# Retention and mixture of experts on one core: y turned in 64x64 quarters of the array, with the order of the loop's VectorE work changed

## The chip, the core and the metric

The kernel runs on one core of a Trainium2 chip. A core has five engines that run side by side, each with its own in-order queue: TensorE (PE, matmuls, with weight loads shown as PEld), VectorE (DVE), ScalarE (ACT), GpSimd (POOL) and SyncE (SP, which here issues most DMAs). Matmuls write to PSUM, everything else lives in SBUF, and 16 DMA engines move data from and to HBM. The metric is the device time of one execution in microseconds.

## The reference, cut to what matters

Inputs: q, k, v of shape (4 batches, 8 heads, 768 steps, 64), a gate of 512 x 8, a noise gate of the same shape, noise, and for 8 experts w1 (512 x 1024) and w2 (1024 x 512), all float32.

```python
# retention with decay: per head h, gamma = 1 - 2 ** (-5 - h)
for t in range(S):
    state = gamma * state + k[t] (x) v[t]            # 64 x 64 per batch and head
    y[t] = (1 / sqrt(64)) * q[t] @ state
x = y.transpose(0, 2, 1, 3).reshape(3072, 512)       # one row per token
# noisy top-2 gating
noisy = x @ w_gate + log1p(exp(x @ w_noise)) * noise
top2 = argpartition(-noisy, 2)[:, :2]; weights = softmax of the two
# experts
for e in range(8):
    out[mask] += weight * (relu(x[mask] @ w1[e]) @ w2[e])
```

## The kernel before

The retention is cut into 24 chunks of 128 steps (`NCH`; 6 chunks per batch, `NC`), and a loop over chunks j does for all 8 heads:

- `qk(j + 1)`: the scores k^T q of the next chunk, 8 float32 matmuls in 64-row tiles, into two PSUM tiles `pA`; VectorE multiplies them with the causal mask into `am`, at the end of `qk` (line 356).
- `x_turn(j - 1)`: the y of the chunk before stands in SBUF as `yt`, with features on partitions and steps along the free dimension. Four matmuls with y as the weights (128x128) and a constant `turn` as the moving operand (144 columns: an identity of 128 and 16 gate columns) put tokens on partitions and give the parts of the logits as well. Behind them four matmuls of one column with bf16 squares `sq` give each token's sum of squares.
- `y_state(j)`: the part of y that comes from the state, 8 matmuls in 64x64 quarters of the array, absent in the first chunk of a batch.
- `x_scale(j - 1)`: two short VectorE operations that make a power of two from the sum of squares (`p2m`, `xsa`).
- `mid[j]`: routing work put in by hand for this chunk (lists filled with `P(j, ...)`), mainly VectorE: top-2 search, one-hot tables, the low halves of w1 (`w_lo_half`), and the DMA transposes `x_t` on SP.
- `load(j + 4)`: q, k, v and kt of chunk j + 4, four DMAs of 256 KB on SP. q is scaled by GpSimd (`q_scale`, two chunks ahead), v as well (`v_scale`, one chunk ahead).
- `x_split(j - 1)`: ScalarE writes the scaled x in f16 and copies the logits' parts, VectorE writes the low half, SP stores both to `xbuf`.
- `todo[j]`: more work put in by hand (loads of weights, gathers of x rows on GpSimd).
- `y_mm(j)`: masked scores times v, 8 matmuls of 128x64; ScalarE copies y to `yt`; 8 matmuls `pU` for the state's update (absent in the last chunk of a batch); ScalarE copies the state to U and squares yt into `sq`.

All engines keep the order of the program text (`tc.manual_schedule()`); semaphores only hold an instruction back. PSUM tiles of the loop (`pY`, `pT`) have one buffer each, `pA` two. The gather of the first expert's rows needs an index that VectorE writes in chunk 18 (`slots`), gathers stand in the `todo` of 18 to 20, and the transposes `x_t` of the gathered rows in 20 and 21. Behind the loop the last turn stands among the first expert's matmuls, and the experts follow, with float16 high and low parts (three matmuls for one product).

## Time and profile before

| | |
|---|---|
| median of 3 runs | 645.42 us (645.26 to 645.45) |
| profiled execution | 645.07 us, its span 643.1 us |
| PE | busy 634.6 us (99%), 4919 matmul records |
| PEld, DVE, ACT, POOL | 390.2, 287.1, 299.8, 202.8 us |
| granted clock of PE | 0.998 of full speed |
| DMA | 113.02 MB, mean 176 GB/s |

The span goes from the first to the last instruction of one profiled execution. A matmul on float32 leaves two records. Busy times of records that overlap are counted once; times on PE are ends that are modelled, starts are read. An idle time on an engine other than PE matters only if PE ends up waiting for it.

### The profile page before, as it was taken

The page shows a single profiled execution, that of the slowest core. Times are in us where ns is not written, and L with a number is a line of the kernel's source. Part 1 is how long each engine was busy: PE and PEld are TensorE (multiplying, and loading weights), DVE is VectorE, ACT ScalarE, POOL GpSimd, SP SyncE. Part 2 cuts the span into 40 slices and gives each one's busy share as a digit, 9 for nine tenths or more (in the row PEclk, how much of TensorE's full clock was granted, in tenths as well). Part 3 has the DMA queues.
Part 4 walks back from the last instruction along what each step waited for, and adds up shares of the span by engine and source line. Part 5 has one row for each costly group of instructions (what it writes and reads, how often), then busy time and mean ns, then how long its engine had stood idle before and what let it go on. Part 6 is the DMA issues. An engine that isn't in the chain of part 4 may idle for free.

```text
span 643.1 us, 12254 instructions
## 1 busy us (share of the span) xinstructions
PE 634.6 (99%) x4919; PEld 390.2 (61%) x4919; DVE 287.1 (45%) x740; ACT 299.8 (47%) x559; POOL 202.8 (32%) x166
## 2 busy tenths in 40 slices
PE   9999999999999999999999999999999999999995
PEld 6999998559578544554455445544554465455574
DVE  4678785897454221654162226222622262215020
ACT  6577457615552443554354344434543454344121
POOL 4555472041540134104410433043304320430214
PEclk9999999999999999999999999999999999999999
DMA  8999999988768067736774577447654794572303
GB/s 301 391 391 375 321 314 277 368 194 296 167 127 276 10 124 131 238 79 97 143 205 131 100 129 203 142 87 130 190 162 83 126 209 144 95 126 45 50 10 43
DMA packets 94423, 113.02 MB, mean 176 GB/s; under 512 B 60662, under 2 KB 61820, under 8 KB 90780
## 3 DMA queue, kind: packets, MB, share of 16 engines
q1 hardware_dynamic: 82576, 85.57, 43.6%
q0 software_dynamic: 11776, 26.63, 22.9%
q8 instruction: 40, 0.66, 0.4%
q14 instruction: 19, 0.16, 0.1%
q10 hardware_dynamic: 12, 0.01, 0.0%
HBM read 72.66 MB, written 26.42 MB: 154 GB/s over the span
## 4 chain that ended last, share of the span: by engine, by line
PE 97%; ACT 1%; DVE 1%; issue 0%; POOL 0%; POOLq 0%; ACTq 0%
PE pH L873 13%; PE pH L874 13%; PE pH L875 13%; PE pO L919 12%; PE pO L921 12%; PE pO L920 12%; PE pA L353 4%; PE pT L401 4%; PE pY L375 4%; PE pT L975 2%; PE pY L368 2%; PE pO L963 2%; PE pU L384 1%; PE pO L951 1%; PE pO L950 1%; PE pO L949 1%
## 5 line engine op out<-in xcount | busy, mean ns | idle before, releaser
L910 POOL DMA_INDIRECT out<-ot,idx x51 | 83.6, 1639 | 321.6 <-ACT ot L905 190.2
L873 PE MATMUL pH<-xe,w1h 128*128 128x384 f16 (+5 forms) x576 | 180.9, 314 | 0.0
L875 PE MATMUL pH<-xe,w1l 128*128 128x384 f16 (+5 forms) x576 | 180.9, 314 | 0.0
L874 PE MATMUL pH<-xe,w1h 128*128 128x384 f16 (+5 forms) x576 | 180.8, 314 | 0.0
L882 DVE SCALAR_TENSOR_TENSOR hl<-pH,hh 128x384 f16<-128x384 f32 (+5 forms) x144 | 75.6, 527 | 139.7 <-ACT hh L879 139.0
L921 PE MATMUL pO<-w2h,hl 128*128 128x512 f16 x344 | 130.4, 379 | 0.0
L920 PE MATMUL pO<-w2l,hh 128*128 128x512 f16 x344 | 130.4, 379 | 0.0
L919 PE MATMUL pO<-w2h,hh 128*128 128x512 f16 x344 | 130.4, 379 | 0.0
L879 ACT ACTIVATE hh<-pH 128x384 f16<-128x384 f32 (+5 forms) x144 | 67.1, 467 | 122.7 <-PE pH L875 111.4
L905 ACT ACTIVATE ot<-pO,gse 128x512 f32<-128x512 f32 x45 | 30.9, 687 | 155.2 <-PE pO L921 140.5
L235 DVE SCALAR_TENSOR_TENSOR w1l<-wst,wsc,w1h 128x1024 f16<-128x1024 f32 x28 | 35.9, 1284 | 95.6 <-ACT w1h L230 95.6
L873 PEld LDWEIGHTS <-w1h 128*128 128x128 f16 x576 | 56.3, 98 | 33.0 <-issue 2.7
L875 PEld LDWEIGHTS <-w1l 128*128 128x128 f16 x576 | 56.3, 98 | 30.9
L874 PEld LDWEIGHTS <-w1h 128*128 128x128 f16 x576 | 56.3, 98 | 29.8
L207 ACT ACTIVATE junk<-wst 128x1024 bf16<-128x1024 f32 x64 | 67.2, 1050 | 0.0
L723 POOL DMA_INDIRECT xg<-xbuf,idx x54 | 55.2, 1022 | 30.8 <-issue 12.7
L921 PEld LDWEIGHTS <-hl 128*128 128x128 f16 x344 | 33.7, 98 | 40.6
L919 PEld LDWEIGHTS <-hh 128*128 128x128 f16 x344 | 33.7, 98 | 40.5 <-issue 0.4
L920 PEld LDWEIGHTS <-hh 128*128 128x128 f16 x344 | 33.7, 98 | 39.6
L356 DVE TENSOR_TENSOR am<-pA,mask 128x512 f32<-128x512 f32 x48 | 30.8, 683 | 17.9 <-PE pA L353 17.9
L326 POOL TENSOR_TENSOR vp<-in_v,cs 128x512 f32<-128x512 f32 x24 | 25.1, 1046 | 36.4 <-issue 22.9
L230 ACT ACTIVATE w2h<-wst,wsc 128x1024 f16<-128x1024 f32 x32 | 36.5, 1140 | 0.0
(181 smaller groups left out, 680.5 us busy)
## 6 DMA issues: line engine op xcount, KB each, us to landing
wst<-w SPq DMA_DIRECT2D x28, 1024.0 KB
in_q<-qT SPq DMA_DIRECT2D x24, 256.0 KB
in_k<-kT SPq DMA_DIRECT2D x24, 256.0 KB
in_v<-vt SPq DMA_DIRECT2D x24, 256.0 KB
in_kt<-kt SPq DMA_DIRECT2D x24, 256.0 KB
xbuf<-x SPq DMA_DIRECT2D x24, 256.0 KB
out<-zero SPq DMA_DIRECT2D x6, 1024.0 KB
wst<-w SPq DMA_DIRECT2D x8, 512.0 KB
```

What stands on the lines that cost most here:

```text
L207: nc.scalar.activation(junk, st[:, i * 1024:(i + 1) * 1024], AF.Square, accum_out=ss[:, i:i + 1])
L230: nc.scalar.activation(hi, st[:, i * 1024:(i + 1) * 1024], AF.Copy, scale=sc[:, 0:1])
L723: nc.gpsimd.indirect_dma_start(out=x[:n], out_offset=None, in_=xbuf[:128 + B0 * S] if e == 0 and t < 3 else xbuf, in_offset=bass.IndirectO ...
L873: nc.tensor.matmul(p[:, :n], whi, xh, start=(k == 0), stop=False)
L874: nc.tensor.matmul(p[:, :n], whi, xl, start=False, stop=False)
L875: nc.tensor.matmul(p[:, :n], wlo, xh, start=False, stop=(k == KT - 1))
L879: nc.scalar.activation(hh[:, f, n0:n1], p, AF.Relu)
L882: nc.vector.scalar_tensor_tensor(hl[:, f, n0:n1], p, 0.0, hh[:, f, n0:n1], op0=OP.max, op1=OP.subtract)
L910: nc.gpsimd.indirect_dma_start(out=out, out_offset=bass.IndirectOffsetOnAxis(ap=idx[:n, i:i + 1], axis=0), in_=ot[:n], in_offset=None, com ...
L919: nc.tensor.matmul(p, a, WT["2h"][:, f, :], start=(f == 0), stop=False)
L920: nc.tensor.matmul(p, a, WT["2l"][:, f, :], start=False, stop=False)
L921: nc.tensor.matmul(p, c, WT["2h"][:, f, :], start=False, stop=(f == FT - 1))
```

## The change

The turn of y is done in 64x64 quarters: 16 matmuls, each with a 64x64 piece of y as weights and 80 columns of `turn` (64 of an identity, 16 of the gate); for each of four pieces the two row halves and two column halves of the array. The sums of squares are issued ahead of them, and the squares are made right behind `yt`, before the state's copy. The columns of x come in another order, which w1's rows follow (`PERMX`), and the logits come in four parts instead of two. The masks leave `qk` and stand behind `x_scale`; `mid` stands behind `x_split`. Five low halves of w1 move to other chunks.

```diff
-XW = 128 + 2 * E
+XW = 64 + 2 * E
+PERMX = PERM.reshape(KT, 2, 64).transpose(1, 0, 2).reshape(-1)
 def turn_ident(v):
-            nc.vector.tensor_copy(t[:, :, k, k * 2 * E:k * 2 * E + 128], ident[:, None, :].to_broadcast([128, 2, 128]))
+            nc.vector.tensor_tensor(t[:, :, k, k * 2 * E:k * 2 * E + 64], ident[:, None, :64].to_broadcast([128, 2, 64]),
+                                    ident[:, None, 64:].to_broadcast([128, 2, 64]), op=OP.add)
 def turn_gate(v):
-            nc.vector.tensor_copy(t[:, :, k, 128 - k * 128:XW - k * 128], w[:, :, k])
+            nc.vector.tensor_copy(t[:, :, k, 64 - k * 64:XW - k * 64], w[:, :, k])
 def qk(j):
-        for s in range(2):
-            nc.vector.tensor_tensor(AM[j][:, s], pA[s], mask[:, None, :].to_broadcast([128, HP, C]), op=OP.mult)
+        return pA
+
+    def masked(j, pA, s):
+        nc.vector.tensor_tensor(AM[j][:, s], pA[s], mask[:, None, :].to_broadcast([128, HP, C]), op=OP.mult)
 def y_mm(j):
         nc.scalar.activation(y.rearrange("p (s x) -> p s x", s=2), PY.pop(j)[:, :, :2 * C], AF.Copy)
+        SQ[j] = loads.tile([128, KT, C], BF, name="sq", bufs=1)
+        nc.scalar.activation(SQ[j].rearrange("p n c -> p (n c)"), y, AF.Square)
         if c < NC - 1:
...
             nc.scalar.activation(U[(c + 1) % 2], pU, AF.Copy)
-        SQ[j] = loads.tile([128, KT, C], BF, name="sq", bufs=1)
-        nc.scalar.activation(SQ[j].rearrange("p n c -> p (n c)"), y, AF.Square)
 def x_turn(j):
-        PT[j] = p = t[:, 512 - 2 * XW:512 + 2 * XW]
-        p = p.rearrange("p (s x) -> p s x", s=2)
-        PT[j, "s"] = t[:, 512 + 2 * XW:513 + 2 * XW]
-        y = YT.pop(j)
-        for s in range(2):
-            for g in range(2):
-                nc.tensor.matmul(p[:, s, g * 128:g * 128 + XW], y[:, s, g, :], turn[:, v, 2 * s + g],
-                                 start=(g == 0), stop=True, skip_group_check=True)
+        PT[j] = p = t[:, 512 - 4 * XW:512 + 4 * XW]
+        PT[j, "s"] = t[:, 512 + 4 * XW:513 + 4 * XW]
         q = SQ.pop(j)
         for n in range(KT):
             nc.tensor.matmul(PT[j, "s"], q[:, n], oneb[:, 0:1], start=(n == 0), stop=(n == KT - 1), skip_group_check=True)
-        PT[j, "y"] = PT[j].rearrange("p (n x) -> p n x", x=XW)[:, :, :128]
+        y = YT.pop(j)
+        for n in range(KT):
+            for h in range(2):
+                o = (4 * h + n // 2 * 2) * XW + n % 2 * 64
+                r = slice(h * 64, h * 64 + 64)
+                for m in range(2):
+                    i = slice(m * 64, m * 64 + 64)
+                    nc.tensor.matmul(p[i, o:o + XW], y[r, n // 2, n % 2, i], turn[r, v, n],
+                                     start=(n == 0), stop=True, skip_group_check=True)
+        PT[j, "y"] = PT[j].rearrange("p (n x) -> p n x", x=XW)[:, :, :64]
 def logits(j):
-        nc.scalar.activation(LG[g, "s"][:, j - c0], p.rearrange("p (s x) -> p s x", s=2)[:, :, 128:XW], AF.Copy)
+        nc.scalar.activation(LG[g, "s"][:, j - c0], p.rearrange("p (s x) -> p s x", s=4)[:, :, 64:XW], AF.Copy)
 def route_x(g, c0, c1):
-        ls = LG[g, "s"][:, c0:c1]
-        nc.vector.tensor_tensor(LG[g][:, c0:c1], ls[:, :, 0], ls[:, :, 1], op=OP.add)
+        nc.vector.tensor_reduce(LG[g][:, c0:c1], LG[g, "s"][:, c0:c1].rearrange("p n s e -> p n e s"),
+                                axis=AX.X, op=OP.add)
-    for i, j in ((0, 10), (2, 10), (1, 11), (4, 11), (3, 12), (6, 12), (5, 19), (7, 19)):
+    for i, j in ((0, 10), (2, 10), (4, 11), (6, 12), (1, 18), (3, 19), (5, 19), (7, 21)):
         P(j, w_lo_half, 0, "1", i)
 the loop over j:
+        more = j + 1 < NCH
+        pA = qk(j + 1) if more else None
         if j:
             x_turn(j - 1)
         y_state(j)
...
         if j:
             x_scale(j - 1)
-        for f, a in mid.get(j, []):
-            f(*a)
+        if more:
+            masked(j + 1, pA, 0)
+            masked(j + 1, pA, 1)
         if j < NC - 3:
             q_table(j + 3)
         if j + AHEAD < NCH:
             load(j + AHEAD)
         if j:
             x_split(j - 1)
+        for f, a in mid.get(j, []):
+            f(*a)
         for f, a in todo.get(j, []):
             f(*a)
         y_mm(j)
```

## Rows read from the trace of the kernel before

**Rows 1.** The page's chain that ended last, its shares of the span by engine:
```profile
PE 97%; ACT 1%; DVE 1%; issue 0%; POOL 0%; POOLq 0%; ACTq 0%
```

**Rows 2.** PE's timeline, iteration 13: start us, length us, engine, line, operation:
```profile
62.07 1.16 PE L353 MATMUL pA<-qs,in_k 64*128 64x128 f32 x16
63.17 1.24 PE L401 MATMUL pT<-turn,yt 128*128 128x144 f32 x8
64.25 0.24 PE L405 MATMUL pT<-oneb,sq 128*128 128x1 bf16 x4
64.42 0.67 PE L368 MATMUL pY<-qs,U 64*64 64x128 f32 x16
65.02 1.09 PE L375 MATMUL pY<-am,vp 128*64 128x128 f32 x16
65.94 0.64 PE L384 MATMUL pU<-vp,in_kt 128*64 128x64 f32 x16
66.51 0.72 PE L353 MATMUL pA<-qs,in_k 64*128 64x128 f32 x8
```

**Rows 3.** Table by stage: stretch, its length, busy us (records), clock, DMA share, GB/s:
```profile
30.00:50.00 20.00, 20.00 (x335) 18.15 (x336) 14.23 (x52) 14.56 (x34) 10.33 (x10) 1.00 1.05 390
...
103.00:108.00 5.00, 4.76 (x78) 4.36 (x80) 2.86 (x9) 3.77 (x9) 0.10 (x1) 1.00 1.24 216
108.00:110.00 2.00, 2.00 (x41) 1.57 (x38) 1.79 (x12) 1.29 (x5) 0.11 (x1) 1.00 1.02 389
```

**Rows 4.** PE's timeline, the state part's first three and first four records:
```profile
64.42 0.33 PE L368 MATMUL pY<-qs,U 64*64 64x128 f32 x3
...
64.42 0.34 PE L368 MATMUL pY<-qs,U 64*64 64x128 f32 x4
```

**Rows 5.** PE's timeline: scores of chunks 11 and 21, iteration 12, the expert's first matmul:
```profile
49.83 1.16 PE L353 MATMUL pA<-qs,in_k 64*128 64x128 f32 x16
...
59.33 1.25 PE L401 MATMUL pT<-turn,yt 128*128 128x144 f32 x8
...
60.59 0.98 PE L375 MATMUL pY<-am,vp 128*64 128x128 f32 x14
...
92.97 1.16 PE L353 MATMUL pA<-qs,in_k 64*128 64x128 f32 x16
...
109.73 0.34 PE L873 MATMUL pH<-xe,w1h 128*128 128x384 f16 x1
```

**Rows 6.** ScalarE's timeline where a batch ends (chunk 11): y's copy and its squares:
```profile
58.36 0.60 ACT L379 ACTIVATE yt<-pY 128x512 f32<-128x512 f32 x1 [0.43 <-PE pY L375]
58.99 0.63 ACT L388 ACTIVATE sq<-yt 128x512 bf16<-128x512 f32 x1
```

**Rows 7.** SP's timeline: the issue of chunk 11's q and the eighth issue behind it:
```profile
39.88 0.40 SPq L266 DMA_DIRECT2D in_q<-qT  x1
...
46.47 0.33 SPq L266 DMA_DIRECT2D in_kt<-kt  x1
```

**Rows 8.** GpSimd's timeline: the scaling of q of chunks 11 and 21:
```profile
46.53 1.28 POOL L334 TENSOR_TENSOR qs<-in_q,gq 128x512 f32<-128x512 f32 x1
...
90.60 1.27 POOL L334 TENSOR_TENSOR qs<-in_q,gq 128x512 f32<-128x512 f32 x1
```

**Rows 9.** VectorE's timeline, iteration 16, and the gather's index in iteration 18:
```profile
77.12 1.29 DVE L356 TENSOR_TENSOR am<-pA,mask 128x512 f32<-128x512 f32 x2 [1.15 <-PE pA L353]
...
78.65 0.26 DVE L535 TENSOR_TENSOR posb<-pR,t 128x108 f32<-128x108 f32 x1
...
80.66 0.74 DVE L431 SCALAR_TENSOR_TENSOR x<-pT,xsa,x 128x512 f16<-128x512 f32 x1
...
87.69 0.16 DVE L636 SCALAR_TENSOR_TENSOR idx<-roww 128x3 int32<-128x3 f32 x1
```

**Rows 10.** SP's timeline: the first and the last transpose of the first gathered rows:
```profile
94.87 1.35 SPq L741 DMA_TRANSPOSE xe<-xg  x1
...
102.31 2.22 SPq L741 DMA_TRANSPOSE xe<-xg  x1
```

## The prediction, written before the changed kernel ran

> **What bounds the kernel now.** I read the chain of waits first: 97% of the profiled execution hangs on TensorE (PE) [rows 1]. So a change pays only by what it takes off PE's queue, and only as long as nothing else becomes late there. Then I followed one iteration of the attention loop on PE's timeline [rows 2]: scores `qk`, turn of y (8 records in 1.24 us, since a float32 matmul leaves two), the squares' sums, state part, mask part, state update, next `qk`. Each block begins where the one before ends; the iteration is 66.51 - 62.07 = 4.44 us. [...] Last, the table by stage: from 30 to 50 us PE is busy all of 20 us, but the DMA engines are full as well (share 1.05, 390 GB/s) [rows 3]. That is the second bound, hidden just behind the first.

> **The turn itself.** Before, the stretch from the start of the turn to the state part is 64.42 - 63.17 = 1.25 us [rows 2]. What would 16 quarter matmuls, that is 32 records, take? The trace has quarters already: the state part is 64x64 with 128 columns. Four of its records are over after 0.34 us [rows 4] and all sixteen after 0.67 [rows 2], so a round of four costs 0.33/3 = 0.11. The state update has 64 columns, two tiles side by side, eight rounds within 0.64 [rows 2]; less the last round's tail (0.34 - 0.11 = 0.23 in the state part) that is 0.41/7 = 0.06 a round. Between 64 and 128 columns, 80 come to 0.06 + 0.05 x 16/64 = 0.07 us a round, if four go as freely as two; the upper bound is 0.11 (columns don't matter), which is a rival below.

> The sums now come first. They take 64.42 - 64.25 = 0.17 us today [rows 2]; I give them 0.22, since they now stand behind a change of the array's shape. Then comes a first round, as in the state part: its 65.02 - 64.42 = 0.60 to the next block [rows 2] are two rounds of 0.11 and 0.38 for the first round and the drain before another shape, which I split as 0.18 and 0.20 (an estimate). Seven rounds of 0.07 follow: 0.22 + 0.18 + 0.49 = 0.89. The state part behind it has the same shape and needs no filling: 0.11 - 0.18 = -0.07. So 0.82 for 1.25, **0.43 us per turn**, in 20 iterations: **8.6**. In the three iterations that begin a batch (6, 12, 18) there is no state part; 60.59 - 59.33 = 1.26 us [rows 5] becomes 0.22 + 0.18 + 6 x 0.07 + 0.16 (drain, a little under the 0.20 above, for fewer columns) = 0.98: 3 x 0.28 = **0.8**. The last turn, among the expert's matmuls, changes shape twice: **0.2**. Together 9.6 us less on PE. Bounds: with rounds of 0.11 the 9.6 become about 3.3; with rounds as two pairs of 0.07 they become a loss of 3.4.

> **What comes late then.** (a) The squares now stand before the turn on PE and right behind yt on ScalarE. Where a batch ends there is no state update to cover them: yt starts at 58.36, the squares at 58.99 and end at 59.62 [rows 6]; with 0.06 for the signal PE could go on at 59.68, and its turn began at 59.33 [rows 5]. Price 0.35 x 3 = **1.0**. In other iterations the update (0.57 us longer) covers it with 0.1 to spare, and the copy of U, now last, still has the length of the sums and the turn. Ends: 0 and, if that 0.1 is missed in 20 iterations, 3.

> (b) DMA. The queue is full, so loads land when they do now, however fast PE is. The loads are issued with eight in flight: q of chunk 11 is issued at 39.88, and the eighth issue behind it, at 46.47 [rows 7], comes when that load has landed. GpSimd scales it from 46.53 for 1.28 us [rows 8], so the scores of chunk 11 cannot start before 47.85; they start at 49.83 now [rows 5]. There are 2.0 us to win up to there. Nine turns precede (one at a batch's start, worth 0.28 - 0.35): 8 x 0.43 - 0.07 = 3.4. PE waits for the rest: **1.4** lost. After that the weights' load is through and the queue gains on PE again. Ends: 0.4, if the load comes a microsecond sooner, and 3.4.

> (c) x's scale ahead of the masks costs nothing: the sums end about 1.4 us into the iteration, the masks (1.29, [rows 9]) end near 3.0, and PE needs their PSUM only at 4.0. The low part and then the `mid` work follow. In iteration 16 `mid` is long, 80.66 - 78.65 = 2.01 [rows 9]: 1.4 + 0.3 + 1.3 + 0.7 + 2.0 + 0.3 = 6.0, against an iteration of 4.0 now; VectorE runs over into 17 and the masks of 17 hold PE for some 0.15 at the start of 18. In 18 the gather's index, done at 87.85 [rows 9], now waits behind masks and low part (0.75) and that overhang: about 1.2 us later in its iteration. GpSimd does its gather and then scales chunk 21's q, 90.60 to 91.87 [rows 8], for scores at 92.97 [rows 5]: 1.1 to spare. Of it 1.2 is lost by the index and 0.4 by the two iterations between (one 0.43 shorter, the other not, for it waits for squares), so PE waits about 0.5. With the masks **0.7**; ends 0 and 1.8.

> (d) The transposes of the expert's x are in `mid`, hence now behind the store of x on SP's queue. The first is issued at 94.87, 1.9 us into iteration 20 (92.97); it would go at about +4.2, 2.3 later. The weights' load and the other two transposes (the last issued at 102.31, [rows 10]) queue behind it; the slow stretch that they make (216 GB/s) ends at 108 [rows 3], and the expert's first matmul is at 109.73 [rows 5]: 1.7 to spare. 4 x 0.43 = 1.7 of PE's way to it goes. So the wait lies between 0, if the gather's data has by then left the queue and they run faster, and 2.3. I take **0.7**, nearer to the low end because the queue is free of the gathers by then.

> (e) At nothing: the sum of four logits parts instead of two (four instructions, VectorE, behind the low part); the building of the identity; the moved low halves of w1, which fill iterations 18 to 21 before the expert starts. Behind 110 us the trace is the expert's matmuls without a gap, and all that feeds them moves along.

> **Sum.** 9.6 - 1.0 - 1.4 - 0.7 - 0.7 = 5.8 us less. The profiled execution took 645.07 (span 643.1); the median of the runs is 645.42. I forecast 645.42 - 5.8, about **639.6 us**.

> **Rivals.**
> 1. *A floor per record.* No block above starts its records faster than one in some 0.03 us on average: the state part 0.11/4, the state update 0.06/2. For it: blocks of very different columns meet near that value. Against it: three records of a round are over after 0.33 and the fourth after 0.34 [rows 4], so inside a round the starts lie 0.01 apart. If it holds, a round is 0.11: 20 x (1.25 - 1.10) + 3 x 0.02 + 0.2 = 3.3, less 1.0 for the squares, 0.3 for index and masks, 0.3 for the transposes; no DMA wait. That is 1.7 less: 643.7. [...]
> 2. *Pairs, not fours: slower.* The quarters of one row half read the same turn matrix; if two of the four wait for the others, there are 16 rounds of 0.07: 0.22 + 0.18 + 15 x 0.07 - 0.07 = 1.38 for 1.25, a loss of 0.13 x 20 + 0.28 x 3, and 1.0 for the squares: 4.5 longer, 649.9. It decides from 0.12 per four records on, where the gain no longer pays for the squares. Against it: the state part's rounds [rows 4].
> 3. *DMA holds on.* The loads bind longer (3.4) and the transposes come at their upper end (2.3): 9.6 - 1.0 - 3.4 - 0.7 - 2.3 = 2.2 less, 643.2. For it: the share of 1.05. Against: without weights an iteration moves 1.31 MB, 3.4 us at 390 GB/s, against 4.0 on PE.
> 4. *All covered.* No wait but the squares': 8.6 less, 636.8. It asks for a faster queue than in any stage shown.

> **How the numbers follow.** Chances: forecast 0.50, floor 0.15, pairs 0.08, DMA 0.17, all covered 0.10. The range from 636.8 to 644.3 takes in the forecast with the ends of (a) to (d), DMA, most of the floor, and half of the fully covered case; it leaves out the pairs. 0.2% is 1.3 us, about what a measurement can tell from no change; of the floor's 0.15 some 0.05 lie within it. Faster 0.86, same 0.06, slower 0.08.

> **What would show it.** The turn's 32 records in some 0.8 us and the iterations at 4.0 (rounds of 0.11 or pairs: rivals 1 and 2); a wait of PE for the squares where a batch ends; PE held by the scaled q near iterations 8 to 10 and at 20; the expert's first matmul right behind the last transpose. The forecast is wrong if iterations stay above 4.2 us, or if PE loses more than 5 us to waits before the expert starts.

## The result, and the profile after

The changed kernel took **654.44 us** (median of 4 runs, 653.27 to 656.83) against 645.34 for the kernel before on the same chip: ratio 1.0147, 95% interval 1.0117 to 1.0177. It is 9.1 us slower where 5.8 less was forecast.

TensorE is busy for less time (631.1 us for 634.6), but the end no longer hangs on it alone. The page's chain that ended last, shares by engine, answers to [rows 1]:
```profile
PE 89%; DMA 5%; issue 2%; ACT 1%; DVE 1%; POOL 1%; SPq 0%; POOLq 0%; ACTq 0%; DVEq 0%
```
DMA has 5% of it and "issue", time in which nothing that the profile shows was waited for, 2%.

The turn itself does what was forecast, and a little more. PE's timeline of the changed kernel, iteration 2, answers to [rows 2] (start us, length us, engine, line, operation):
```profile
15.19 1.16 PE L355 MATMUL pA<-qs,in_k 64*128 64x128 f32 x16
16.28 0.25 PE L403 MATMUL pT<-oneb,sq 128*128 128x1 bf16 x4
16.46 0.78 PE L411 MATMUL pT<-turn,yt 64*64 64x80 f32 x32
17.07 0.62 PE L372 MATMUL pY<-qs,U 64*64 64x128 f32 x16
17.62 1.09 PE L379 MATMUL pY<-am,vp 128*64 128x128 f32 x16
18.54 0.63 PE L390 MATMUL pU<-vp,in_kt 128*64 128x64 f32 x16
19.10 0.38 PE L355 MATMUL pA<-qs,in_k 64*128 64x128 f32 x2
```
From the sums to the state part it is 17.07 - 16.28 = 0.79 us where it was 1.25, and the iteration is 19.10 - 15.19 = 3.91 us where it was 4.44: 0.52 less (0.43 was forecast). But few iterations look like this. What PE waited for between 8 and 112 us in the changed kernel (engine, line, what was waited for: us in total, times, longest); the same question has no line at all for the kernel before from 10 to 60 us, and one of 0.2 us from 60 to 112:
```profile
PE pY L372 <- issue: 3.0, 3, 1.9
PE pA L355 <- POOL vp L328: 2.5, 2, 1.3
PE pT L411 <- issue: 2.0, 3, 1.1
PE pY L379 <- issue: 0.7, 1, 0.7
PE pA L355 <- POOL qs L336: 0.5, 1, 0.5
PE pU L390 <- issue: 0.4, 1, 0.4
PE pT L403 <- ACT sq L385: 0.3, 1, 0.3
...
```
Two things stand out: 6.1 us of "issue", and 3.0 us before the scores (`pA`). What stands behind an arrow, or in brackets in a timeline, is what ended the wait as far as the profile can tell; it can name the wrong one.

**Loss 1, "issue".** PE's timeline of the changed kernel, iteration 11:
```profile
56.00 0.78 PE L411 MATMUL pT<-turn,yt 64*64 64x80 f32 x32
56.60 0.27 PE L372 MATMUL pY<-qs,U 64*64 64x128 f32 x1
58.74 0.66 PE L372 MATMUL pY<-qs,U 64*64 64x128 f32 x15 [1.87 <-issue]
```
The state part stops after one record and goes on 2.14 us later, with all its data there. Counted through the trace, this break and the eight others of its kind lie after the same number of PE instructions modulo 256 (193, all of PE's instructions in the trace counted), in whatever part of the iteration that falls. (One wait of "issue", 0.3 us at 95.68, lies elsewhere; its cause stays open.) The DMA records show a packet of the instruction queue once per 256 PE instructions; the page has 44 such packets for 0.72 MB, 16 KB each, so 64 bytes per instruction. Each of these breaks ends 1.3 to 1.6 us after such a packet has ended. The author's reading of these times: PE has run through the instructions it holds and waits for the next 256. A quarter turn is 64 instructions (32 weight loads, 32 matmuls) where the old one has 16, so an iteration has 200 and not 152: 256 last 256/200 x 3.91 = 5.0 us where they lasted 256/152 x 4.44 = 7.5. The next packet starts up to 4.3 us after PE has entered a block of 256, moves for 1.0 and is used 1.3 to 1.6 later: up to 6.6 us. That is hidden behind 7.5 us and not behind 5.0. Not every block of 256 shows it: nine of the first thirteen do, and none behind 82 us.

**Loss 2, VectorE late for the scores.** Timelines of PE, VectorE and GpSimd in the changed kernel, iterations 20 to 22 (in brackets the idle time before, and what ended it):
```profile
99.77 0.53 PE L411 MATMUL pT<-turn,yt 64*64 64x80 f32 x20
...
100.36 0.16 DVE L427 TENSOR_SCALAR p2m<-pT 128x1 int32<-128x1 int32 x1 [0.94 <-PE pT L411]
...
100.63 1.28 DVE L360 TENSOR_TENSOR am<-pA,mask 128x512 f32<-128x512 f32 x2
...
101.83 0.74 DVE L438 SCALAR_TENSOR_TENSOR x<-pT,xsa,x 128x512 f16<-128x512 f32 x1
...
102.08 0.98 POOL L730 DMA_INDIRECT xg<-xbuf,idx  x1 [0.16 <-issue]
102.48 2.95 DVE L461 TENSOR_TENSOR sp<-sp,nz 128x48 f32<-128x48 f32 x1
...
103.09 1.05 POOL L328 TENSOR_TENSOR vp<-in_v,cs 128x512 f32<-128x512 f32 x1
104.09 1.27 POOL L336 TENSOR_TENSOR qs<-in_q,gq 128x512 f32<-128x512 f32 x1
...
106.39 1.28 DVE L360 TENSOR_TENSOR am<-pA,mask 128x512 f32<-128x512 f32 x2
...
107.33 1.61 PE L355 MATMUL pA<-qs,in_k 64*128 64x128 f32 x16 [1.19 <-POOL vp L328]
```
VectorE first stands idle 0.94 us in front of x's scale (`p2m`), with the masks (`am`, as long as in [rows 9]) queued behind it. What it waits for is the end of the turn (L411, at 100.30) and not the sums, though these stand first now and were over at 99.58. In every undisturbed iteration `p2m` starts 0.07 us behind the turn's modelled end, 2.13 us into the iteration and 0.78 behind the end of the sums. So the masks end about 3.7 us into an iteration of 3.9, and little of what comes behind them fits in. Then the mid work, now behind the low part, falls beside GpSimd's work: `sp<-sp,nz`, 48 elements, takes 2.95 us and ends when GpSimd's `qs` does, at 105.4. In the kernel before it took 0.24:
```profile
95.69 0.24 DVE L454 TENSOR_TENSOR sp<-sp,nz 128x48 f32<-128x48 f32 x1
```
The next masks come only at 106.39, and the scores, which need their PSUM, at 107.33. The "POOL vp" in the bracket is not the cause, for the scores do not read `vp`; at the start of iterations 17, 18 and 22 they come 0.93 to 0.94 us behind the start of `am`, wherever `vp` stands. That GpSimd's work holds VectorE here is read from these times; the run without v's scaling tests it.

**Loss 3, the way to the expert.** Issues on SP, ScalarE and PE in the changed kernel, ends of the loop:
```profile
103.04 1.57 SPq L748 DMA_TRANSPOSE xe<-xg  x1
...
104.66 1.10 SPq L204 DMA_DIRECT2D wst<-w  x2
...
110.36 1.06 ACT L208 ACTIVATE junk<-wst 128x1024 bf16<-128x1024 f32 x1 [1.57 <-DMA wst<-w]
...
113.40 0.25 PE L403 MATMUL pT<-oneb,sq 128*128 128x1 bf16 x4 [1.63 <-ACT sq L385]
```
The first transpose went at 94.87 [rows 10], now at 103.04, behind the store of x; the load of w2 stands behind it, and ScalarE waits for that load with everything behind it. Behind this gap PE runs below full clock, as the table by stage of the changed kernel shows (columns as in [rows 3]):
```profile
112.00:114.00 2.00, 0.60 (x28) 0.59 (x32) 1.22 (x4) 1.97 (x7) 0.00 (x0) 1.00 1.16 230
114.00:119.00 5.00, 5.00 (x71) 3.33 (x61) 2.62 (x14) 3.67 (x8) 0.19 (x1) 0.66 0.90 299
```
A granted clock of 0.66 over these 5 us is a mixture: 0.50 for 3.4 us, from 115.2 to 118.6, and 1.00 before and behind that. The break of 2.14 us in iteration 11 was followed by no such stretch (1.00 from 50 to 80 us).

**The account.** Taken from the starts of PE's blocks, iteration by iteration against the kernel before, up to the start of iteration 22 (107.33 against 101.84, 5.5 later, 0.4 of which was there at the start of iteration 1):

| iterations 1 to 21 | us |
|---|---|
| turn, sums and state part shorter, 18 x 0.52 and 3 x 0.36 where a batch begins | -10.4 |
| PE out of instructions (iterations 3, 4, 6, 7, 9, 10, 11, 14, 15) | +8.6 |
| scores wait for VectorE's masks (7, 13, 16, 17, 18, 21) | +4.3 |
| scores wait for the scaled q (chunk 11, 0.2; chunk 21, 0.5) | +0.7 |
| sums wait for the squares where a batch ends (6, 12) | +0.7 |
| the rest, 0.65 of it the break at 95.68 | +1.2 |

In iteration 18 the squares cost nothing: they end at 89.92, and the scores, late for their masks, hold the sums until 90.29.

Another 1.5 us are lost up to the expert's first matmul (116.75; 109.73 in [rows 5]), and 1.2 behind it, since the spans differ by 8.2.

### The profile page after: what moved, and what is told of

It is laid out like the page before. It is cut to its first block, busy times and chain, and to the rows that moved or that the text cites. A ratio compares the mean times of both kernels' runs of the same rounds, so it can differ in the third digit from the quotient of the medians.

```text
span 651.3 us, 13441 instructions
## 1 busy us (share of the span) xinstructions
PE 631.1 (97%) x5495; PEld 383.1 (59%) x5495; DVE 296.9 (46%) x740; ACT 302.1 (46%) x559; POOL 207.5 (32%) x166
## 4 chain that ended last, share of the span: by engine, by line
PE 89%; DMA 5%; issue 2%; ACT 1%; DVE 1%; POOL 1%; SPq 0%; POOLq 0%; ACTq 0%; DVEq 0%
PE pH L885 13%; PE pH L887 13%; PE pH L886 13%; PE pO L931 11%; PE pO L933 11%; PE pO L932 11%; PE pA L355 3%; PE pY L379 2%; PE pT L987 2%; PE pT L411 2%; PE pO L975 2%; DMA xbuf<-x 1%; DMA in_q<-qT 1%; DMA in_kt<-kt 1%; DMA wst<-w 1%
## 5 line engine op out<-in xcount | busy, mean ns | idle before, releaser
L730 POOL DMA_INDIRECT xg<-xbuf,idx x54 | 57.8, 1070 | 38.0 <-issue 12.5
L231 ACT ACTIVATE w1h<-wst,wsc 128x1024 f16<-128x1024 f32 x32 | 36.1, 1137 | 0.1
L236 DVE SCALAR_TENSOR_TENSOR w2l<-wst,wsc,w2h 128x1024 f16<-128x1024 f32 x28 | 35.7, 1275 | 0.0
```

Source lines behind the costliest of these rows:

```text
L231: nc.scalar.activation(hi, st[:, i * 1024:(i + 1) * 1024], AF.Copy, scale=sc[:, 0:1])
L236: nc.vector.scalar_tensor_tensor(lo, st[:, i * 1024:(i + 1) * 1024], sc[:, 0:1], hi, op0=OP.mult, op1=OP.subtract)
```

## The experiments

Each kernel is named with its median and its ratio to the kernel before on the same chip. Where a run is said to be so many us late or early, starts on PE's timeline are compared with those of the kernel before.

**The quarter turn alone** (x's scale, masks, mid work, squares and low halves of w1 as before). Edit, against the kernel after:
```diff
-        if j: x_scale(j - 1)
-        if more: masked(j + 1, pA, 0); masked(j + 1, pA, 1)
+        # masks inside qk, x_scale, then mid, then load and x_split
-        q = SQ.pop(j) ... sums        # ahead of the turn
+        ... sums                      # behind the turn
```

> The kernel before with the quarter turn alone: squares behind the state's copy, sums behind the turn, masks, mid work and low halves of w1 as before. Theory: two separate losses, TensorE running out of fetched instructions while the DMA queues are full, and VectorE's mid work moved behind the masks, beside GpSimd. Here only the first remains: the turn saves about 9.6 us, gaps at every 256th TensorE instruction up to 77 us cost about 7.5, and the 100-us stretch is clean: about 643 us. Rival A (the fetch gaps are a by-product, only the new order costs): no such gaps, 636 to 638 us. Rival B (the order is harmless, the fetch and what follows from it cost all): 650 or more.

Measured: 649.31 us, 1.0067 (1.0045 to 1.0089), slower by 4.1. 643 was expected. Undisturbed iterations are 0.36 us shorter than in the kernel before (the sums now stand behind). What PE waited for, 10 to 60 us and then 60 to 112:
```profile
PE pA L355 <- POOL qs L336: 1.8, 2, 1.4
PE pY L370 <- issue: 1.1, 1, 1.1
PE pT L406 <- issue: 0.9, 1, 0.9
PE pT L406 <- DVE x L436: 0.9, 1, 0.9
PE pY L377 <- issue: 0.4, 1, 0.4
...
PE pY L370 <- issue: 1.9, 2, 1.3
PE pA L355 <- issue: 0.9, 1, 0.9
...
```
"Issue" has 5.5 us (the last 0.3 in a row left out) without any of the new order, and the scores no longer wait for masks: the two losses are separate, as the theory had it. Its time missed by 6 us, and lies near rival B's. The breaks do not end at 77 us, the last is at 111.73; the turn saves 0.36 an iteration and not 0.43; and two waits were not expected: 1.8 us for the late q of chunks 9 and 10, and 0.9 for the building of the second identity, which the prediction had at nothing. VectorE adds two halves of the identity where it copied one, beside GpSimd again, and holds the low part of x and with it the turn:
```profile
23.92 1.04 POOL L328 TENSOR_TENSOR vp<-in_v,cs 128x512 f32<-128x512 f32 x1 [1.80 <-PE pU L386]
23.96 2.43 DVE L305 TENSOR_TENSOR turn<-ident 128x128 f32<-128x128 f32 x2
24.92 1.32 POOL L336 TENSOR_TENSOR qs<-in_q,gq 128x512 f32<-128x512 f32 x1
...
29.89 0.53 PE L406 MATMUL pT<-turn,yt 64*64 64x80 f32 x17 [0.85 <-DVE x L436]
```

**The new order alone**, with the old turn of 16 instructions behind the sums:
```diff
-        for n in range(KT): for h in range(2): for m in range(2): ... 64x64 quarters
+        for s in range(2):
+            for g in range(2): nc.tensor.matmul(p[:, s, ...], y[:, s, g, :], turn[:, v, 2 * s + g], ...)
```

> The kernel after with the old turn (16 records of 144 columns), but with all of the new order: sums and squares first, x's scale ahead of the masks, mid work behind the low part, low halves moved. Theory: TensorE issues as few instructions as before, so no gap at every 256th; VectorE's mid work still runs beside GpSimd's scaling and the transposes still stand behind the store: TensorE waits between 80 us and the expert, some 8 us in all with the squares: about 653 us. Rival A (order alone): the same 653. Rival B (fetch alone): 646, the squares' 1.0 us and nothing else.

Measured: 653.46 us, 1.0109 (1.0078 to 1.0139). No break at every 256th instruction; the order alone costs 8.2 us, as expected. Up to iteration 22 it is 4.9 us late: squares 0.7, scores behind the masks 2.7, behind the scaled q of chunk 21 0.7, the start 0.3, and 0.5 in small pieces. From there to the expert 4.4 more, nearly all in one place on PE's timeline and in a stretch of lower clock behind it (0.83 from 110 to 120 us, as much as 3.4 us at 0.50):
```profile
...
114.38 0.25 PE L403 MATMUL pT<-oneb,sq 128*128 128x1 bf16 x4 [3.15 <-DVE mb L484]
```
The chain of waits leads back from there over the low and high part of x and ScalarE's sum of w2's squares to the load of w2, issued at 104.60 behind the transpose and landed at 111.34. Turn alone and order alone cost 4.1 and 8.2 us, together 9.1 and not 12.3: with quarters the sums in front save 0.16 more in each iteration (0.52 for 0.36), which neither run has.

**The new order, transposes put back** ahead of the loads and the store:
```diff
-    P(20, x_t, 0, 0); P(21, x_t, 0, 1)
+    P(20, x_t, 0, 0, d=ahead); P(21, x_t, 0, 1, d=ahead)   # run ahead of load and x_split
```

> The new order with the old turn, with one thing put back: the first two transposes of the expert's x are issued ahead of the chunk's loads and store again, not behind the store. Theory: the loads of w2 behind them on SyncE's queue are issued some 2 us earlier, so ScalarE's sum of w2's squares no longer holds the high part of x and with it TensorE: of that run's gap of 3.4 us before the expert, and the slow clock behind it, 3 us go: about 650 us. Rival (the load's length in the queues, not its issue, sets its end): 653, as without it.

Measured: 651.00 us, 1.0091 (1.0075 to 1.0108). The load of w2 is issued at 102.37, not 104.60, the idle time of 3.15 us before the last turns shrinks to 0.90 with no slow clock behind it (mean granted clock of the profiled execution 0.997, in the run before it 0.994), and the expert's first matmul comes at 115.08, not 119.01. The medians differ by 2.5 us where 3 was expected; the runs of the two overlap (650.73 to 654.61 without, 650.49 to 651.88 with it), so the traces carry this more than the times.

**The same without GpSimd's scaling of v** (v's tiles also get one more buffer):
```diff
-        VP[j] = loads.tile(...); nc.gpsimd.tensor_tensor(VP[j], IN["v", j], vtab, op=OP.mult)
+        VP[j] = IN["v", j].rearrange("p (h d) -> p h d", h=H)
```

> The run with the new order, the old turn and the transposes put back, now without GpSimd's scaling of v: the matmuls take the loaded tile, so v goes unscaled; GpSimd has 1.04 us less in each iteration, the rest is the same. Theory: VectorE's mid work stands still while GpSimd writes, in iterations 15 to 20 for up to 2.9 us at once; with only the scaling of q left it is held less and the scores' waits for masks in iterations 15 to 20 (0.48, 1.28, 0.45 and 0.75 more per iteration than before) at least halve: 1.5 to 3 us less than that run, 648 to 649.5. Rival (VectorE's work is simply too long there, whatever GpSimd does): the waits stay, 651.

Measured: 648.55 us, 1.0049 (1.0034 to 1.0064), 2.5 less than the run before it. One and the same VectorE operation, 12 elements in iteration 17, in the run with v's scaling and in the one without:
```profile
83.49 1.18 DVE L559 TENSOR_SCALAR lb<-si 128x12 int32<-128x12 int32 x1
```
```profile
82.44 0.17 DVE L557 TENSOR_SCALAR lb<-si 128x12 int32<-128x12 int32 x1
```
Of the waits in iterations 15, 17, 18 and 19 (0.48, 1.28, 0.45 and 0.75) only 0.34 in 18, the squares' at a batch end, is left; 0.46 for masks in 21 is new. The first three were waits for masks, and the hold by GpSimd is their cause, not the length of VectorE's work. The 0.75 was one for the scaled q of chunk 21 (scaled until 97.17, scores at 97.22); it may also be gone because GpSimd's own queue is 1.04 us shorter.

**The kernel after with the mid work at its old place**, ahead of the load and of x's parts:
```diff
+        for f, a in mid.get(j, []): f(*a)
         if j < NC - 3: q_table(j + 3)
         ... load, x_split
-        for f, a in mid.get(j, []): f(*a)
```

> The kernel after with one loop moved back: the mid work stands again ahead of the load's issue and of the high and low parts of x, though behind the masks. Theory: the fetch gaps stay (about 7.5 us, most before 77 us); of the waits between 80 us and the expert most go, since the mid work runs earlier in the iteration and the transposes stand ahead of the store again: about 647 us. Rival A (order alone): 640. Rival B (fetch alone): within 1 us of the kernel after, 654.

Measured: 658.32 us, 1.0202 (1.0185 to 1.0219): all three theories missed. What PE waited for between 8 and 112 us:
```profile
PE pT L403 <- DVE x L438: 6.7, 8, 2.6
PE pT L403 <- DVE cum L553: 3.3, 1, 3.3
...
```
The sums cannot write before the low part of x has read the one buffer `pT`, and now sums, x's scale, masks, mid work and low part form one ring, with `mb` and `den` held by GpSimd to 1.03 and 1.23 us in it. In the kernel before the masks fill the time in which the sums are still to come; the ring is shorter by them. Most of the loss is in two places: the sums wait 2.57 us in iteration 15 and 3.29 in 17, and the clock is low for several us behind either (0.50 from 78 to 82 us, 0.52 from 92 to 96). "Issue" has only 2.1 us here, likely because iterations that other waits hold use fewer instructions in the same time.

**The kernel after with the masks in front of x's scale:**
```diff
-        if j: x_scale(j - 1)
-        if more: masked(j + 1, pA, 0); masked(j + 1, pA, 1)
+        # masks at the end of qk(j + 1), as before
+        if j: x_scale(j - 1)
```

> The kernel after with the masks put back ahead of x's scale in VectorE's order; the mid work stays behind the low part, and all else is as after. Theory: with x's scale in front, VectorE stands still until the sums are there, and the masks and all behind them come some 1.3 us later; with the masks in front, the scores no longer wait for masks in iterations 17 to 22, where the kernel after lost about 3 us: about 651.5 us, the fetch gaps still there. Rival A (the mid work beside GpSimd is what is late, wherever the masks stand): 654, no change. Rival B (the low part, now behind the masks, frees the turn's buffer later): 656 or more.

Measured: 658.16 us, 1.0193 (1.0176 to 1.0210): rival B. What PE waited for, its first two lines:
```profile
PE pT L401 <- ACT sq L383: 6.6, 8, 1.1
PE pA L355 <- POOL qs L336: 3.3, 4, 1.3
```
ScalarE's copy of y and its squares stand behind the high part of x, and that waits for x's scale, which now has the masks and the mid work of the iteration before ahead of it. So the two moves of the order cannot be judged one by one: with the quarters, either one alone takes 658 us, both 654, and none 649 (with sums and squares at their old places as well).

**The kernel after without the load of k by rows** (v's tiles also get one more buffer):
```diff
+            if n == "kt": IN[n, j] = IN["v", j]; continue
```

> The kernel after without the load of k by rows: the state's update multiplies with v's tile instead, so 256 KB less are loaded in each iteration, and the state is another one; instructions of TensorE are the same in number and shape. Theory: TensorE's instruction fetch waits behind the full DMA queues, so the gaps at every 256th instruction vanish or shrink to under 0.3 us each: some 7 us less than the kernel after, about 647, with the waits between 80 us and the expert still there. Rival (the fetch has a latency of its own, whatever the queues carry): the gaps stay at 0.3 to 1.4 us, and the time stays within 1.5 us of the kernel after.

Measured: 648.60 us, 1.0060 (1.0039 to 1.0081), 5.8 less than the kernel after. "Issue" has two lines between 8 and 112 us, where the kernel after had 6.1 us:
```profile
PE pY L382 <- issue: 0.7, 1, 0.7
PE pT L414 <- issue: 0.2, 1, 0.2
```
All four breaks left (two too short for these lines) lie before 45 us, where w1 still loads and the DMA share is 0.98 (30 to 50 us). Behind 50 us it is 0.68 to 0.84 up to 100, the next packet starts 0.5 to 2.2 us after PE has entered a block of 256, and there is none. So the fetch is quicker where the DMA engines carry less. The load is not all of it: in the kernel before, at a share of 1.02 to 1.05 up to 70 us, the packets started 1.1 to 2.6 us after. The other waits do not go: 2.1 us for masks and 1.8 for squares, and 2.7 for q and k that come late.

**The turn alone in pairs:** each record takes both column halves, the same rounds with half the instructions, 168 per iteration.
```diff
-                for m in range(2):
-                    i = slice(m * 64, m * 64 + 64)
-                    nc.tensor.matmul(p[i, o:o + XW], y[r, n // 2, n % 2, i], turn[r, v, n], ...)
+                nc.tensor.matmul(p[:, o:o + XW], y[r, n // 2, n % 2, :], turn[r, v, n], ...)
```

> The turn alone once more, as in the run with the quarter turn alone, but each record takes both column halves: 64 rows by 128 columns of the array, 16 records two side by side, where the quarters were 32 records four side by side. Rounds and columns are the same, TensorE's instructions per iteration 168, where the quarters have 200 and the turn before has 152. Theory (the quarters' instructions outrun the fetch): the turn is as short as with quarters, gaps at every 256th instruction are gone or under 1 us in all; what stays is the late q near iteration 8, about 1.6 us, the second identity's 0.8 and some 0.5 elsewhere: about 642 us. Rival A (the gaps come with the shorter iteration, whatever the count): no better than the quarters alone, 649. Rival B (only four side by side are quick): a turn of 1.36 us and 648 or more.

Measured: 646.29 us, 1.0018 (0.9992 to 1.0044), 10 runs from 643.72 to 650.96. What PE waited for between 8 and 128 us:
```profile
PE pT L404 <- DVE x L434: 4.4, 2, 3.7
PE pA L355 <- POOL qs L336: 1.5, 3, 0.7
...
```
"Issue" is gone: it was the number of instructions. 256 of them last 6.4 us here (168 in 4.21), 5.2 with the quarters alone (200 in 4.08), and of that difference the longer iteration makes only 0.2. 642 us was expected: the rounds of two start 0.105 us apart, not 0.07, so the iteration is only 0.22 shorter than before. The 3.7 us in the list are the late load of w2 once more (issued at 97.46, landed at 106.47, beside two transposes that held SP 4.17 and 3.83 us); that run took 649.85.

**Pairs with sums ahead and the identity from ScalarE:**
```diff
+        if c < NC - 1: sums()            # ahead of the turn, behind it where a batch ends
+        if v: nc.scalar.activation(t[:, :, k, r], f[:, :, k, r], AF.Copy)   # second identity
```

> The pairs of the run beside it, with two more changes. The sums stand ahead of the turn and the squares ahead of the state's copy, except for the chunk that ends a batch, whose sums stay behind the turn; and the second identity is copied by ScalarE from the first, not added by VectorE. VectorE's order is that of the kernel before. Theory: one change of the array's shape less, 0.16 us in each of 16 iterations, and 0.7 for the identity: some 3 us less than the pairs alone, about 639 us. Rival (the wait for the late q near iteration 8 takes it back, or the squares make the turn wait): within 1 us of the pairs alone.

Measured: 646.20 us, 1.0022 (1.0010 to 1.0033): no better than the pairs alone, as the rival has it. Iterations are 0.02 us shorter than before, not 0.22. The sums, 128 rows by 128 columns, stand here between scores and pairs, which both are 64 by 128. Without them in between the scores take 1.00 us to the next block and the pairs 0.95, with them 1.09 and 1.05; with quarters the same move brought 0.16.

**Pairs, calmed:** the second identity from ScalarE, the first two sums of w2 one iteration later.
```diff
-            at0(21 + i, w_sum, 0, "2", i)
+            at0(22 + i, w_sum, 0, "2", i)
```

> The pairs alone, with two of their late places mended: the second identity is copied by ScalarE from the first (VectorE's addition took 2.4 us beside GpSimd and held the turn 0.7), and ScalarE's first two sums of w2's squares stand one iteration later, so that a late load of w2 no longer holds the high part of x. Theory: in the runs of the pairs that were not held there, 643.7 to 644.7 us were measured; with 0.7 less for the identity about 643.3, and the runs no longer spread to 650. Rival (the time lost at the load of w2 comes back at the expert's second layer): 645 or more.

Measured: 645.64 us, 1.0014 (0.9996 to 1.0032), 643.3 expected; eleven of twelve runs lie between 644.68 and 647.17, one took 651.78. The expert's first matmul comes 1.6 us earlier than before, and the wait for w2's sums takes it back on PE:
```profile
113.78 0.16 PE L218 MATMUL pR<-wsb,oneb 128*128 128x4 bf16 x1 [1.33 <-ACT wsb L214]
```

**Two more on the loads.** Both start from the calmed pairs. First, w1's loads are spread:
```diff
-        at(3 + i, w_load, 0, "1", i)
+        at((3, 5, 6, 8)[i], w_load, 0, "1", i)   # sums, high and low halves up to two iterations later
```

> The run beside it, with the four loads of w1 spread over iterations 3, 5, 6 and 8 instead of 3 to 6, and the work on them up to two iterations later. Theory: the scores' waits for the late q near iterations 8 and 9, about 1.1 us, come from the four loads in a row on full queues; spread, they shrink by a microsecond: 642.3 us. Rival (the queues are full of the chunks' own loads, so any place costs the same, or the later low halves of w1 delay VectorE): no better than the run beside it, or up to 1 us slower.

Measured: 648.76 us, 1.0051 (1.0032 to 1.0071). Iteration 8 starts 1.3 us early and not late, but the later low halves of w1 hold the turn 2.1 us in three places, 1.6 of it in iteration 13, with the granted clock at 0.50 for 3.4 us behind it (mean of the profiled execution 0.994). That is worse than theory and rival. Then w2's loads are issued earlier:
```diff
-        at((20, 20, 21, 21)[i], w_load, 0, "2", i)
+        at((17, 18, 20, 21)[i], w_load, 0, "2", i)   # first two sums back in 21 and 22
```

> The calm pairs with the first three loads of w2 issued earlier, in iterations 17, 18 and 20 instead of 20, 20 and 21, and the first two sums of w2's squares back in iterations 21 and 22. Theory: what the calm pairs won in the loop, 1.6 us up to the expert's first matmul, was lost at the wait for the sums of w2, 1.65 us, because the loads crawl beside the transposes; issued where the queues carry 250 GB/s they are there in time, and the gain stays: about 643.8 us, less than either kernel. Rival (the loads' bytes only change places: the last chunks' loads or the gathers come later by as much): 645.3 or more.

Measured: 649.29 us, 1.0067 (1.0048 to 1.0086). The one profiled execution took 644.37 and has no wait for w2's sums; the five others took 647.51 to 651.19 and have no trace, so what they lost stays open. That is in the rival's range. No version beats the kernel before; the pairs alone and the calmed pairs cannot be told from it.

## Why the prediction was wrong

- **The turn's price was right**, with 0.52 for 0.43 per iteration (10.4 us up to iteration 21 for 8.6); the floor and the pairs of rivals 1 and 2 did not occur. Rounds of four start 0.07 us apart, as forecast.
- **The step that failed first is one that has no term in it:** "Together 9.6 us less on PE" prices array time alone. The 48 instructions that each iteration gains were never costed in fetching. They take 8.6 us in the kernel after, and show as 5.5 us of "issue" with the turn alone and none with half the instructions. The count could be read from the trace of the kernel before: 76 weight loads and 76 matmuls an iteration, so with 48 more, 256 instructions last 5.1 us at the forecast 4.0 us an iteration, where they lasted 7.5. So could a packet of the instruction queue that starts up to 2.7 us after a block of 256 is entered, and takes 1.0; these 3.7 us would still have fitted. What that trace could not show is the 1.3 to 1.6 us from the packet's end to its use, and that packets start up to 4.3 us late beside the quarters.
- **(c), "x's scale ahead of the masks costs nothing ... With the masks 0.7":** masks and scaled q cost 5.0 us in the kernel after (4.3 and 0.7), 3.4 with the order alone. The 0.5 for chunk 21's q came as forecast. The masks' part failed in two steps. The sum starts with "the sums end about 1.4 us into the iteration", but x's scale waits for the end of the turn behind them and starts at 2.13, so the masks end at 3.7 and not "near 3.0". And the prediction let VectorE's operations keep the lengths they had in their old place: moved beside GpSimd's scaling they took up to 2.95 us for 0.24, and without v's scaling one of 1.18 us (`lb`) is back at 0.17.
- **(d), 0.7 for the transposes:** the place was right, the size not. Put back, they gave 2.5 us between the medians. Their range was reckoned up to the expert's x; what bound was the load of w2 behind them, through ScalarE's queue, and then the clock (0.83 from 110 to 120 us with the order alone).
- **(a), 1.0 for the squares:** right where they bind, 0.35 in each of iterations 6 and 12, and 0.7 in all; in the run without v's scaling 18 binds too, and it is 1.0. **(b), 1.4 for the late q:** 1.8 with the turn alone, which is luck. "Loads land when they do now" did not hold: there chunk 11's q is issued at 43.43 us for 39.88 and scaled from 49.96 for 46.53, and it is the q of chunks 9 and 10 that PE waits for. Why the queue fell behind stays open. In the kernel after PE came late by then and 0.2 shows.
- **(e)** had the identity at nothing; with the turn alone it cost 0.9. The moved low halves of w1 (three of them, 1, 3 and 7, and not five) cost nothing that shows. "All that feeds them moves along" failed too: 1.2 us more were lost behind the expert's first matmul.

Open: what decides how long the packet waits in a given block of 256 beyond the DMA's load, which breaks a lower clock follows, and why runs of the pairs spread by 7 us where the kernel before spreads by 2.

## What to carry to other kernels

Where matmuls are cut into smaller ones, count the instructions per microsecond as well as the columns: 256 of them have to last longer than a fetch, here up to 6.6 us (at a DMA share of 0.96, from 50 to 60 us). A short VectorE operation need not keep its length when it is moved beside GpSimd (48 elements took 2.95 us for 0.24), so read what GpSimd does at the new place. And an in-order queue whose head waits (x's scale, here with VectorE idle for 0.94 us) should have filling work ahead of it, not behind; what ends its wait is to be read from the trace, here the turn and not the sums that it reads.
